# Attention and two feed-forward layers on one core: keys rotated by a block, half-empty blocks transposed in pairs, narrower value products

## The chip, the cores and the metric

The kernel runs on one core of a Trainium2 chip. The metric is device time in microseconds (us); the median of three timed runs is given, and the profile is of one further execution with its own time. Engines are named as the profile names them: PE (matrix products and transposes), PEld (its weight loads), DVE, ACT, POOL, and SP, which issues most DMA.

## The reference

```python
# q, k, v: (4, 8, 576, 64)  -> 32 heads of 576 positions, 9 blocks of 64
scores = (1.0 / np.sqrt(64)) * np.matmul(q, k.transpose(0, 1, 3, 2))
scores = np.where(pos[:, None] // 64 >= pos[None, :] // 64, scores, -1000000000.0)
attn = softmax(scores)                       # over the last axis
x = heads_side_by_side(np.matmul(attn, v))   # (2304, 512)
h = np.maximum(x @ w_in, 0.0);  x = h * h @ w_out            # d_ff 2048
h = x @ w_in2                                                # second layer
g = (a0 + a1 * h + a2 * h**2 + a3 * h**3) / (1 + abs(b0 * h) + abs(b1) * h**2 + 1e-6)
out = g @ w_out2
```

A query sees the keys of its own block of 64 and of all blocks before it.

## The kernel before, in words

**Queries.** Each head's 576 queries are padded in front with 64, which makes five tiles of 128 (t = 0 to 4). Tile t holds the query blocks 2t-1 and 2t. Its upper 64 rows see key blocks 0 to 2t, its lower 64 rows all of these but the last. So tile t has 128t + 64 columns of scores, and the last 64 of them are of use to the upper rows alone; for the others the score is masked.

**Slots.** A head is four slots (the table `GROUPS`): tiles 0 and 1 together, then tile 2, tile 3, tile 4. A slot passes through scores (`emit_s`, PE), row maxima (`emit_max`, DVE), exponentials with row sums (`emit_exp`, ACT, into tiles called p), scaling by the reciprocal of the sum (`emit_norm`, POOL), transposes of p in blocks of 128 by 128 through a PSUM tile tp (`emit_t`, PE), and copies into one tile pt that holds p with keys on the partitions. `emit_pv` then multiplies values by pt: half 0 covers the queries of tiles 0 to 2, half 1 those of tiles 3 and 4.

**Three rounds.** Heads 0 to 7 run in round one with slots 0 and 1 only and in round two with slots 2 and 3. Heads 8 to 31 run in round three with all four. Heads 0 to 9 are "plain": products in fp32, pt is `pt_plain`, one ACT copy per piece, and two heads share a value product's array side by side. The 22 others are "split": every number is a high and a low fp32r part, ACT copies the high part into pt and DVE writes the rest as the low part, and each value product is run for both (z = 0, 1).

**Buffers.** There are two sets of p tiles. The second lies in a pool `early` that is given up at the start of round three for `q_two` and `k_two`, so round three has one p tile for each t, whatever the head (`psets[un.hd % 2 if un.hd < H else 0]`; in the trace all are called p). pt exists once.

**Order.** `tc` schedules by a model of its own, so the order on every engine is the scheduler's; each engine then runs its list in order. Between the attention products PE runs the first half of the first feed-forward layer for the batch before (`moe_a`: tiles ha and ya, lines L482 and L495), a given number of steps for each slot. After attention come the rest of `moe_a` for the last batch, the second half of the layer (hb, yb) and the second layer (hc, yc). While attention runs, ACT, DVE and POOL also convert the layer's weights (tiles raw, cv, w).

Of the kernel before, what the change touches and what calls it, by code (L numbers as in the profile page):

```python
# [49 lines left out]
def attention_moe_moe(ctx: ExitStack, tc: tile.TileContext, q, k, v, wi1, wo1, wi2, wo2, a, b, out):  # L50
# [89 lines left out]
    early = tc.alloc_tile_pool(name="early", bufs=1)  # L140
    psets = []
    for pool in (attn, early):
        psets.append([])
        for t in range(5):
            w_ = P * (t + 1)
            pt_ = pool.tile([P, w_], F32, name=f"p{t}_{len(psets)}")
            nc.gpsimd.memset(pt_[:, w_ - D:w_], 0.0)
            if t == 0:
                nc.gpsimd.memset(pt_[0:D, 0:D], 0.0)
            psets[-1].append(pt_)  # L150


        nc.gpsimd.memset(psets[-1][3][:, D:P], 0.0)
        nc.gpsimd.memset(psets[-1][3][0:D, 0:D], 0.0)
        for n in (3, 4):
            nc.gpsimd.memset(psets[-1][n][:, SUB:SUB + D], 0.0)

    def ptile(un, t):
        own = psets[un.hd % 2 if un.hd < H else 0]
        if un.gis == (0, 1) and un.hd % 4 > 1:  # L160
            return own[4][:, 0:3 * P] if t == 2 else own[3][:, P * t:P * (2 * t + 1)]
        return own[t]

    pt = attn.tile([P, 2, 3, SP], F32, tag="pt", name="pt_plain", bufs=1)

# [6 lines left out]
    class Visit:  # L172
        def __init__(self, n, hd, at, gis):
            self.n, self.hd, self.plain, self.at, self.gis = n, hd, hd < PLAIN, at, gis

            self.scale = SCALE if n == 0 else 1.0

            self.q0, self.q1 = (0, 3 * P) if gis == (0, 1) else (3 * P, SP) if gis == (2, 3) else (0, SP)
            self.k1 = SUB if gis == (0, 1) else S

    def load_qk(un, eng=nc.sync):
# [8 lines left out]
        cuts = ((0, 256, 0, 192), (256, un.q1, 192, un.k1)) if un.n == 0 else ((un.q0, un.q1, 0, un.k1),)  # L190
# [9 lines left out]
    def make_two(un):  # L200
        early.release()
        late = tc.alloc_tile_pool(name="late", bufs=1, reuse_waits="tile")
        for n in range(2):
            q_two.append(late.tile([P, SP], F32R, name=f"q_two{n}"))
            k_two.append(late.tile([P, S], F32R, name=f"k_two{n}"))
            nc.scalar.activation(q_two[n][D:P], un.qr[D:P], AF.Copy)
            nc.scalar.activation(k_two[n][D:P], un.kr[D:P], AF.Copy)
        return late
# [57 lines left out]
    def emit_s(i):  # L266
# [12 lines left out]
        for t in g:  # L279
# [9 lines left out]
            else:  # L289
                o = D if t == 1 else 0  # L290
                parts = [(ps[:, o:o + w_], 0, w_)]
# [13 lines left out]
    def p_view(i, t):  # L305
        pv = ptile(slots[i][0], t)[D if t == 0 else 0:P, 0:P * t + D]
# [26 lines left out]
    def emit_norm(i):  # L333
# [19 lines left out]
        for n, t in enumerate(g):  # L353
            r = D if t == 0 else 0
            pv = ptile(slots[i][0], t)[r:P, 0:P * t + D]
            nc.gpsimd.tensor_scalar(pv, pv, st[r:P, 6 + n:7 + n], 0.0, op0=ALU.mult, op1=ALU.add)  # L356

    def emit_t(i):
# [3 lines left out]
        if un.hd == PLAIN and gi == 0:  # L362
            pt = attn.tile([P, 2, 3, SP], F32R, tag="pt", name="pt", bufs=1)
        un.pt = pt
        blocks = [(t, c) for t in g for c in range(t + 1)]
        for lo in range(0, len(blocks), 4):
            part = blocks[lo:lo + 4]
            ps = ps1.tile([P, 512], F32, tag="tp", name=f"tp{i}_{lo}", bufs=3)
            for n, (t, c) in enumerate(part):
                nc.tensor.transpose(ps[:, P * n:P * (n + 1)], ptile(slots[i][0], t)[:, P * c:P * (c + 1)], ident)  # L370
            t = g[-1]
            here, late = slice(P * t, P * (t + 1)), slice(P * (t - 3), P * (t - 2))

            if gi == 0:
                moves = [(slice(D, 2 * P), 0, slice(D, 2 * P)), (slice(2 * P, 3 * P), 1, slice(P, 2 * P))]
            elif lo:
                moves = [(slice(0, P), 1, slice(0, P))]
            else:
                moves = [(slice(0, 3 * P), None, here)]
                if gi > 1:  # L380
                    moves.append((slice(3 * P, 4 * P), 2, late))
            if un.plain:
                for src, c, cols in moves:
                    piece, dst = ps[:, src], un.pt[:, un.hd % 2, slice(0, 3) if c is None else c, cols]
                    if c is None:
                        piece = piece.rearrange("p (c j) -> p c j", j=P)
# [5 lines left out]
            ends = []  # L392
# [492 lines left out]
```

## Time and profile before

| | us |
|---|---|
| median of three runs | 1023.35 (1022.27 to 1026.43) |
| profiled execution, its own time | 1018.61 |
| its span, first to last instruction | 1016.8 |

A row of groups gives line, engine, operation, output<-inputs, shape and count, then busy us and mean ns of one, then idle us of the engine before them and what ended it. In a timeline each row begins with its start and its length in us. On PE, products follow each other while the earlier ones are still under way, so that the time one takes from its engine is the distance between starts, not its length. A fp32 product stands as two records in the trace, a transpose and a fp32r product as one.

### The profile page before, as it was taken

What the parts mean: (1) busy time and instruction counts of PE and PEld (TensorE: products, weight loads), DVE (VectorE), ACT (ScalarE), POOL (GpSimd) and SP (SyncE); (2) the same over time, 40 slices, a digit from 0 to 9 for tenths busy, and PEclk for the clock granted to TensorE, in tenths of its full rate; (3) what the DMA queues carried; (4) which work ended last, traced back from release to release, by engine and by line L of the source; (5) the groups of instructions that cost most, each with busy time, mean ns of one, the idle gap of its engine ahead of it and who ended that gap; (6) DMA issues with size and microseconds to landing.
All of it is one profiled execution on the core that took longest, in us unless ns stands there. A gap on an engine that the chain in (4) does not pass through costs nothing. (4 is left out here: it accounts for less than half of the span.)

```text
span 1016.8 us, 17069 instructions
## 1 busy us (share of the span) xinstructions
PE 995.1 (98%) x5721; PEld 882.6 (87%) x5721; DVE 741.8 (73%) x1412; ACT 728.5 (72%) x1620; POOL 591.1 (58%) x632
## 2 busy tenths in 40 slices
PE   7999999999999999999999999999999999999997
PEld 5678998999999999999888888887888888899996
DVE  6799688768787756676676756887766766777766
ACT  6789697768787746664555557887787776787775
POOL 4767686868786845630232448767556554655552
PEclk9999999999999999999999999999999999999999
DMA  8866435243332204567656572001101100100000
GB/s 268 253 195 216 128 97 154 88 114 116 119 93 81 67 24 141 191 193 256 231 166 200 172 242 88 1 1 42 41 1 32 42 1 1 57 17 1 32 1 31
DMA packets 63894, 106.58 MB, mean 105 GB/s; under 512 B 16064, under 2 KB 34496, under 8 KB 63808
## 3 DMA queue, kind: packets, MB, share of 16 engines
q1 hardware_dynamic: 63520, 105.34, 32.7%
q8 instruction: 45, 0.74, 0.3%
q14 instruction: 41, 0.34, 0.1%
q10 hardware_dynamic: 288, 0.16, 0.1%
HBM read 79.17 MB, written 23.07 MB: 101 GB/s over the span
## 5 line engine op out<-in xcount | busy, mean ns | idle before, releaser
L816 PE MATMUL yc<-w_co,gc 128*128 128x512 f32 x864 | 211.6, 391 | 2.9 <-ACT gc L776 2.9
L707 PE MATMUL hc<-xc,w_ci 128*128 128x512 f32 (+1 forms) x960 | 211.2, 368 | 0.0
L707 PEld LDWEIGHTS hc<-xc,w_ci 128*128 128x128 f32 x960 | 176.1, 188 | 26.3
L816 PEld LDWEIGHTS yc<-w_co,gc 128*128 128x128 f32 x864 | 161.2, 188 | 35.5 <-ACT gc L776 4.4
L777 POOL TENSOR_TENSOR gc<-t,gc 128x512 fp32r<-128x512 f32 (+1 forms) x78 | 105.1, 1353 | 126.1 <-issue 103.2
L482 PE MATMUL ha<-xt,w_ai 128*128 128x320 f32 (+1 forms) x768 | 122.5, 305 | 0.5 <-POOL xt L451 0.5
L495 PE MATMUL ya<-ga,w_ao 128*128 128x320 f32 (+1 forms) x768 | 116.8, 299 | 1.6 <-ACT r L508 0.9
L802 POOL TENSOR_TENSOR wq<-wq,ab 128x512 f32<-128x512 f32 (+1 forms) x78 | 96.3, 1235 | 28.6 <-ACT wq L800 28.6
L482 PEld LDWEIGHTS ha<-xt,w_ai 128*128 128x128 f32 x768 | 107.6, 189 | 5.1 <-issue 3.0
L495 PEld LDWEIGHTS ya<-ga,w_ao 128*128 128x128 f32 x768 | 106.5, 189 | 3.5 <-ACT r L508 1.1
L747 PE MATMUL yb<-gb,w_bo 128*128 128x512 f32 (+1 forms) x480 | 106.0, 368 | 0.0
L707 PE MATMUL hb<-xb,w_bi 128*128 128x512 f32 (+1 forms) x480 | 105.7, 368 | 0.0
L776 ACT ACTIVATE gc<-t 128x512 fp32r<-128x512 f32 (+1 forms) x80 | 47.1, 589 | 73.0 <-DVE t L785 72.9
L803 DVE TENSOR_TENSOR t<-hc,t 128x512 f32<-128x512 f32 (+1 forms) x80 | 50.9, 637 | 66.1 <-ACT t L801 66.1
L747 PEld LDWEIGHTS yb<-gb,w_bo 128*128 128x128 f32 x480 | 87.6, 188 | 12.0 <-DVE yp L752 0.3
L707 PEld LDWEIGHTS hb<-xb,w_bi 128*128 128x128 f32 x480 | 87.4, 188 | 11.3 <-ACT yo L500 0.2
L356 POOL TENSOR_SCALAR p<-p,stat 64x64 f32<-64x64 f32 (+4 forms) x110 | 64.4, 586 | 44.2 <-DVE stat L352 11.1
L402 DVE TENSOR_TENSOR pt<-tp,pt 128x128 fp32r<-128x128 f32 (+2 forms) x176 | 63.2, 391 | 27.0 <-ACT pt L400 16.6
L783 DVE SCALAR_TENSOR_TENSOR wq<-wq,ab 128x512 f32<-128x512 f32 (+1 forms) x80 | 54.9, 687 | 33.5 <-ACT ab L782 22.2
L370 PE MATMUL tp<-ident,p 128*128 128x128 f32 x480 | 77.8, 278 | 0.5 <-ACT xp L437 0.3
L400 ACT ACTIVATE pt<-tp 128x128 fp32r<-128x128 f32 (+2 forms) x176 | 57.1, 362 | 26.6 <-PE tp L370 25.0
L785 DVE SCALAR_TENSOR_TENSOR t<-t,coef,ab 128x512 f32<-128x512 f32 (+1 forms) x80 | 66.8, 835 | 1.7
(137 smaller groups left out, 2004.8 us busy)
## 6 DMA issues: line engine op xcount, KB each, us to landing
kr<-in_k_dram SPq DMA_DIRECT2D x32, 288.0 KB, 3.6
raw_ci<-in_wi_dram SPq DMA_DIRECT2D x16, 512.0 KB, 4.1
raw_co<-in_wo_dram SPq DMA_DIRECT2D x16, 512.0 KB, 3.9
qr<-in_q_dram SPq DMA_DIRECT2D x24, 320.0 KB, 3.3
raw_ai<-in_wi_dram SPq DMA_DIRECT2D x8, 512.0 KB, 5.1
raw_ao<-in_wo_dram SPq DMA_DIRECT2D x8, 512.0 KB, 4.0
raw_bi<-in_wi_dram SPq DMA_DIRECT2D x8, 512.0 KB, 3.4
raw_bo<-in_wo_dram SPq DMA_DIRECT2D x8, 512.0 KB, 3.5
```

What stands on the lines that cost most here:

```text
L356: nc.gpsimd.tensor_scalar(pv, pv, st[r:P, 6 + n:7 + n], 0.0, op0=ALU.mult, op1=ALU.add)
L370: nc.tensor.transpose(ps[:, P * n:P * (n + 1)], ptile(slots[i][0], t)[:, P * c:P * (c + 1)], ident)
L400: nc.scalar.activation(high, src, AF.Copy)
L402: nc.vector.tensor_tensor(low, src, f(high), op=ALU.subtract)
L482: nc.tensor.matmul(ps[:, 0:n], w[:, zw, P * kk:P * (kk + 1)], xt[:, zx, kk, first:end], start=i == 0, stop=i == 3 * KK - 1)
L495: nc.tensor.matmul(ps[:, 0:n], wA["o", m][:, zw, P * c:P * (c + 1)], gs[m][:, zg, 0:n], start=i == 0, stop=i == 3 * HALF - 1)
L707: nc.tensor.matmul(ps[:, 0:n], w[:, zw, P * kk:P * (kk + 1)], xt[:, zx, kk, 0:n], start=i == 0, stop=i == 3 * KK - 1)
L747: nc.tensor.matmul(acc[j, c][:, 0:n], wB["o", m][:, zw, P * c:P * (c + 1)], g[:, zg, 0:n], start=m == 0 and i == 0, stop=last and i == 2)
L777: (nc.vector if u - 2 >= len(units) - END else nc.gpsimd).tensor_tensor(g[:, 1, 0:n], t, f(g[:, 0, 0:n]), op=ALU.subtract)
L785: nc.vector.scalar_tensor_tensor(t, t, a0, r, op0=ALU.add, op1=ALU.mult)
L802: (nc.vector if u >= len(units) - END else nc.gpsimd).tensor_tensor(w, w, ab, op=ALU.mult)
L816: last = nc.tensor.matmul(acc[j, c], g[:, zg, P * c:P * (c + 1)], w3["o", m][:, zw, :], start=m == 0 and i == 0, stop=m == NM - 1 and i == 2)
```

## The change

1. The keys in memory are rolled by one block: column 0 holds block 8, then blocks 0 to 7. Tiles 0 to 3 read them from column 64 on. Tile 4 then has its half-used block first and not last.
2. p tiles lie side by side so that two half-used blocks of 64 columns share one 128 by 128 transpose: that of tile 0 with that of tile 1, that of tile 3 with that of tile 4. A head has 13 transposes instead of 15. A shared block is copied into pt in two pieces of 64 by 64, the second of them from partitions 64 to 127 to partitions 0 to 63; group (0, 1) has three copies instead of two, tile 3 one instead of two, tile 4 four instead of three.
3. The zeros that such copies no longer bring are written once into pt (`clear_pt`), and again when pt changes type at head 10.
4. Two sets of p tiles for tiles 0 to 2, three for tiles 3 and 4 in round two, two in round three. The pools `early` and `late` are gone.
5. Value products leave out columns whose p is zero: the two narrow ones of each half go from 256 and 128 columns to 192 and 64.

```diff
+    firsts = [attn.tile([P, 2 * P], F32, name=f"p01_{n}") for n in range(2)]
+    thirds = [attn.tile([P, 3 * P], F32, name=f"p2_{n}") for n in range(2)]
+    rests = [attn.tile([P, 8 * P], F32, name=f"p34_{n}") for n in range(3)]
...
+    def homes(un):
+        n = un.hd % 2
+        if un.gis == (0, 1):
+            if un.hd % 4 > 1:
+                return rests[n][:, 0:2 * P], rests[n][:, 2 * P:5 * P], None
+            return firsts[n], thirds[n], None
+        return firsts[n], thirds[n], rests[(un.hd + 2) % 3 if un.gis == (2, 3) else 1 - n]
...
+    def pblock(un, t, c):
+        first, third, rest = homes(un)
+        if t < 2:
+            return first[:, 0:P] if c < t else first[:, P:2 * P]
+        if t == 2:
+            return third[:, P * c:P * (c + 1)]
+        at = P * c if t == 3 else P * (c + 4)
+        return rest[:, at:at + P] if c < t else rest[:, 3 * P:4 * P]
...
-        blocks = [(t, c) for t in g for c in range(t + 1)]
+        t = g[-1]
+        blocks = [(t, c) for c in range(t + (t < 3))]
+        if t == 4:
+            blocks.append((4, 4))
+        up, low, mid = slice(0, D), slice(D, P), slice(P + D, 2 * P)
...
             if gi == 0:
-                moves = [(slice(D, 2 * P), 0, slice(D, 2 * P)), (slice(2 * P, 3 * P), 1, slice(P, 2 * P))]
+                moves = [(P, slice(0, P), 0, here), (up, mid, 1, mid), (low, mid, 0, low)]
             elif lo:
-                moves = [(slice(0, P), 1, slice(0, P))]
+                moves = [(up, low, 2, low), (low, low, 1, low)]
             else:
-                moves = [(slice(0, 3 * P), None, here)]
-                if gi > 1:
-                    moves.append((slice(3 * P, 4 * P), 2, late))
+                moves = [(P, slice(0, 3 * P), None, here)]
+                if t == 4:
+                    moves.append((P, slice(3 * P, 4 * P), 2, slice(P, 2 * P)))
...
     PV = (
-        ((0, D, 0, 320), (1, P, D, 256), (2, 2 * P, 192, P)),
-        ((0, 384, 0, 256), (1, 384, 0, 256), (2, 384, 0, 256), (3, 0, 0, 256), (4, 0, P, P)),
+        ((0, D, 0, 320), (1, P + D, P, 192), (2, 2 * P + D, 2 * P, D)),
+        ((0, 384, 0, 256), (1, 384, 0, 256), (2, 384, 0, 256), (3, D, D, 192), (4, D, P + D, D)),
     )
...
-        "k": stack(k, 0, MASKED),
+        "k": np.roll(stack(k, 0, MASKED), d_, axis=2),
```

The scheduler orders the instructions anew. Two places on PE show how.

PE in round three, from the last scores of slot 60 (head 15, tiles 0 and 1) on; tp is named by its slot. Before:

```order
L294 MATMUL sy60_2176<-k_two1_1140,q_two1_1139 128x192
L495 MATMUL ya0_1_0_2134<-ga0_1_4_1948,w_ao4_1100 128x256 x3
L495 MATMUL ya0_1_0_2134<-ga0_1_5_2013,w_ao5_1185 128x256 x3
L495 MATMUL ya0_1_0_2134<-ga0_1_6_2068,w_ao6_1264 128x256 x3
L370 MATMUL tp55_4_2106<-ident_70,p4_1_100 128x128
L442 MATMUL pv13_1_2142<-pt_1438,vs13_1931 128x256 x4
L442 MATMUL pv13_1_2142<-pt_1438,vs13_1931 128x128
L442 MATMUL pv13_1_2142<-pt_1438,vs13_1931 128x256 x4
L370 MATMUL tp56_0_2159<-ident_70,p0_1_91 128x128
L370 MATMUL tp56_0_2159<-ident_70,p1_1_94 128x128 x2
```

Of the change, the same place:

```order
L305 MATMUL sy60_2151<-k_two1_1113,q_two1_1112 128x192
L506 MATMUL ya0_1_0_2108<-ga0_1_4_1922,w_ao4_1077 128x256 x3
L506 MATMUL ya0_1_0_2108<-ga0_1_5_1988,w_ao5_1156 128x256 x3
L506 MATMUL ya0_1_0_2108<-ga0_1_6_2040,w_ao6_1236 128x256 x3
L387 MATMUL tp52_0_1945<-ident_70,p01_1_89 128x128 x2
L453 MATMUL pv12_1_1931<-pt_1409,vs12_1719 128x192
L453 MATMUL pv12_1_1931<-pt_1409,vs12_1719 128x64
L387 MATMUL tp53_0_1979<-ident_70,p2_1_91 128x128 x3
L305 MATMUL sx61_2182<-kk15_2000,qh15_1999 128x320
```

Before, the transposes of head 14 (slot 56, three of them) follow the scores of slot 60 and read the same p tiles that slot 60's exponentials write. Now those of head 13 stand there (slot 52, two of them), in a tile that slot 60 uses again after them; slot 56 comes later, from another tile.

PE at the end of attention, from the value product of head 31's first half on (ha3 is feed-forward work of the last batch). Before:

```order
L442 MATMUL pv31_0_5341<-pt_1438,vs31_5262 128x320
L442 MATMUL pv31_0_5341<-pt_1438,vs31_5262 128x256
L442 MATMUL pv31_0_5341<-pt_1438,vs31_5262 128x128
L370 MATMUL tp126_0_5354<-ident_70,p3_1_98 128x128
L370 MATMUL tp127_0_5379<-ident_70,p4_1_100 128x128 x4
L482 MATMUL ha3_0_1_5466<-xt3_4275,w_ai1_349 128x320
L482 MATMUL ha3_0_3_5506<-xt3_4275,w_ai3_512 128x320 x9
L370 MATMUL tp127_4_5388<-ident_70,p4_1_100 128x128
L482 MATMUL ha3_0_1_5466<-xt3_4275,w_ai1_349 128x320 x2
L482 MATMUL ha3_0_3_5506<-xt3_4275,w_ai3_512 128x320 x2
L442 MATMUL pv31_1_5404<-pt_1438,vs31_5262 128x256 x4
```

Of the change:

```order
L453 MATMUL pv31_0_5316<-pt_1409,vs31_5236 128x320
L453 MATMUL pv31_0_5316<-pt_1409,vs31_5236 128x192
L453 MATMUL pv31_0_5316<-pt_1409,vs31_5236 128x64
L387 MATMUL tp127_0_5351<-ident_70,p34_0_92 128x128 x4
L387 MATMUL tp127_4_5360<-ident_70,p34_0_92 128x128
L453 MATMUL pv31_1_5378<-pt_1409,vs31_5236 128x256 x3
L453 MATMUL pv31_1_5378<-pt_1409,vs31_5236 128x192
L453 MATMUL pv31_1_5378<-pt_1409,vs31_5236 128x64
L453 MATMUL pv31_1_5378<-pt_1409,vs31_5236 128x256 x3
L493 MATMUL ha3_0_1_5439<-xt3_4250,w_ai1_334 128x320 x2
```

The 14 feed-forward products that stood between head 31's last transposes and its last value product now stand elsewhere.

## Rows read from the trace of the kernel before

**Rows 1.** The page: span, and busy time by engine.
```profile
span 1016.8 us, 17069 instructions
PE 995.1 (98%) x5721; PEld 882.6 (87%) x5721; DVE 741.8 (73%) x1412; ACT 728.5 (72%) x1620; POOL 591.1 (58%) x632
```

**Rows 2.** Windows of 50 us: length, busy us (count) by engine, PE clock, DMA.
```profile
50.00:100.00 50.00, 49.41 (x319) 38.28 (x317) 47.52 (x80) 43.69 (x123) 35.64 (x39) 1.00 0.68 203
150.00:200.00 50.00, 46.42 (x358) 44.95 (x358) 40.11 (x116) 37.53 (x110) 35.78 (x49) 1.00 0.41 123
250.00:300.00 50.00, 50.00 (x394) 49.83 (x392) 40.30 (x115) 39.90 (x120) 39.32 (x55) 1.00 0.38 113
```

**Rows 3.** Windows of 10 us in round two, columns as in rows 2.
```profile
70.00:80.00 10.00, 10.00 (x65) 7.33 (x65) 9.78 (x19) 8.74 (x28) 6.37 (x8) 1.00 0.52 150
80.00:90.00 10.00, 9.41 (x67) 7.46 (x65) 9.49 (x16) 9.90 (x27) 5.48 (x6) 1.00 0.64 204
```

**Rows 4.** Timeline of PE: a run of five transposes.
```profile
44.56 0.71 PE L370 MATMUL tp<-ident,p 128*128 128x128 f32 x5
```

**Rows 5.** Timeline of PE in round three.
```profile
305.94 0.19 PE L294 MATMUL sy<-kk,qh 128*128 128x64 f32 x1
...
306.26 0.28 PE L294 MATMUL sy<-k_two,q_two 128*128 128x192 f32 x1
306.37 0.27 PE L370 MATMUL tp<-ident,p 128*128 128x128 f32 x1
...
307.07 0.64 PE L442 MATMUL pv<-pt,vs 128*128 128x256 f32 x4
307.54 1.04 PE L495 MATMUL ya<-ga,w_ao 128*128 128x320 f32 x6
308.42 0.49 PE L370 MATMUL tp<-ident,p 128*128 128x128 f32 x3
...
309.05 0.81 PE L442 MATMUL pv<-pt,vs 128*128 128x128 f32 x6
309.69 0.51 PE L370 MATMUL tp<-ident,p 128*128 128x128 f32 x3
```

**Rows 6.** Groups by line and shape, whole span.
```profile
L370 PE MATMUL tp<-ident,p 128*128 128x128 f32 x480 | 77.8, 278 | 0.5 <-ACT xp L437 0.3
L402 DVE TENSOR_TENSOR pt<-tp,pt 128x384 fp32r<-128x384 f32 x66 | 36.4, 552 | 16.7 <-PE tp L370 6.9 <-ACT pt L400 6.5 <-PE pv L442 2.3
L400 ACT ACTIVATE pt<-tp 128x384 fp32r<-128x384 f32 x66 | 32.3, 490 | 18.5 <-PE tp L370 17.6
L402 DVE TENSOR_TENSOR pt<-tp,pt 128x128 fp32r<-128x128 f32 x88 | 24.5, 280 | 2.8 <-ACT pt L400 2.7
L400 ACT ACTIVATE pt<-tp 128x128 fp32r<-128x128 f32 x88 | 24.1, 274 | 7.7 <-PE tp L370 7.4
L429 PE MATMUL pv<-pt_plain,vs 128*64 128x256 f32 x100 | 18.4, 390 | 0.0
L294 PE MATMUL sx<-kr,qr 128*128 128x288 f32 x40 | 11.6, 412 | 0.1
L294 PE MATMUL sy<-kr,qr 128*128 128x448 f32 x20 | 9.6, 564 | 0.5 <-ACT p L328 0.3
L445 ACT ACTIVATE tmp<-pv 64x320 f32<-64x320 f32 x22 | 9.5, 432 | 3.7 <-PE pv L442 3.2
```

**Rows 7.** What PE waited for from 150 to 200 us: us in total, times, longest.
```profile
PE sy L294 <- ACT p L328: 2.7, 2, 1.5
```

**Rows 8.** Timeline of all engines around the second of these waits.
```profile
180.88 0.49 PE L370 MATMUL tp<-ident,p 128*128 128x128 f32 x3
...
181.24 0.31 ACT L328 ACTIVATE p<-sy,stat 64x64 f32<-64x64 f32 x1 [3.47 <-issue]
...
183.29 0.47 PE L294 MATMUL sy<-kk,qh 128*128 128x448 f32 x1 [1.21 <-ACT p L328]
```

**Rows 9.** Timelines of POOL and PE at the start.
```profile
2.75 0.23 POOL L156 MEMSET p<- 128x64 f32 x2
...
3.58 2.48 PE L294 MATMUL sy<-kr,qr 128*128 128x64 f32 x6 [3.58 <-DMA kr<-in_k_dram]
```

More of the change, by code (lines that the diff above doesn't have):

```diff
@@ L158, in ptile @@
-    def ptile(un, t):
[L159 to L162, printed above, removed]
+    firsts = [attn.tile([P, 2 * P], F32, name=f"p01_{n}") for n in range(2)]
+    thirds = [attn.tile([P, 3 * P], F32, name=f"p2_{n}") for n in range(2)]
+    rests = [attn.tile([P, 8 * P], F32, name=f"p34_{n}") for n in range(3)]
+    for n in range(2):
+        for z, o in ((firsts[n], 0), (rests[n], 0)):
+            nc.gpsimd.memset(z[0:D, P + D:2 * P], 0.0)
+        for z, o in ((thirds[n], 0), (rests[n], 2 * P)):
+            nc.gpsimd.memset(z[:, o + SUB:o + 3 * P], 0.0)
@@ L164, in attention_moe_moe, with clear_pt @@
+    def ptile(un, t):
+        first, third, rest = homes(un)
+        if t < 2:
+            return first[:, 0:P + D] if t else first[:, P + D:2 * P]
+        return third[:, 0:SUB] if t == 2 else rest[:, 0:3 * P + D] if t == 3 else rest[:, 3 * P + D:8 * P]
+    def clear_pt(z):
+        nc.gpsimd.memset(z[D:P, :, 0, D:P], 0.0)
+        nc.gpsimd.memset(z[D:P, :, 1, D:2 * P], 0.0)
+        nc.gpsimd.memset(z[D:P, :, 2, D:P], 0.0)
     pt = attn.tile([P, 2, 3, SP], F32, tag="pt", name="pt_plain", bufs=1)
+    clear_pt(pt)
@@ L368, in emit_t @@
             ps = ps1.tile([P, 512], F32, tag="tp", name=f"tp{i}_{lo}", bufs=3)
[L369 to L372, printed above, removed]
+            for n, (_, c) in enumerate(part):
+                nc.tensor.transpose(ps[:, P * n:P * (n + 1)], pblock(un, t, c), ident)
             if gi == 0:
[L375 removed]
+                moves = [(P, slice(0, P), 0, here), (up, mid, 1, mid), (low, mid, 0, low)]
             elif lo:
[L377 removed]
+                moves = [(up, low, 2, low), (low, low, 1, low)]
             else:
[L379 to L381 removed]
+                moves = [(P, slice(0, 3 * P), None, here)]
+                if t == 4:
+                    moves.append((P, slice(3 * P, 4 * P), 2, slice(P, 2 * P)))
+            ends = []
+            for rows, src, c, cols in moves:
+                piece = ps[:, src] if rows is P else ps[rows, src]
+                dst = [(un.pt[:, z] if rows is P else un.pt[up, z])[:, slice(0, 3) if c is None else c, cols]
+                       for z in ((un.hd % 2,) if un.plain else range(2))]
+                ends.append((piece.rearrange("p (c j) -> p c j", j=P) if c is None else piece, dst))
             if un.plain:
[L383 to L386, printed above, removed]
+                for piece, (dst,) in ends:
                     if gi != 0 or un.hd < H:
@@ L601, in attention_moe_moe @@
         if i == 4 * PLAIN - 4:
-            late = make_two(slots[i][0])
+            make_two(slots[i][0])
         for back in range(4):
```

48 lines of the change are left out of this document (12 added, 36 removed).

## The prediction

> **What bounds the kernel now.** I read the page first: PE is busy for 98% of the span, and no other engine for more than 73% [rows 1]. A busy PE need not be a full one, so I read the windows next. From 250 to 300 us, with split heads in round three, PE has 394 products and transposes in 50 us and never pauses, while DVE, ACT and POOL have 10 us to spare each [rows 2]. There a product that goes away is time gained, and the feed-forward stages behind wait for PE alone. Two stretches of attention are different. From 50 to 100 us DVE is busy for 47.5 of 50 us, and PE gets only 319 products done [rows 2]; in round two DVE has 9.78 and 9.49, and ACT up to 9.90, of every 10 us [rows 3]. PE counts as busy there but is not the limit. And from 150 to 200 us PE stands idle for 3.6 us [rows 2], of which 2.7 are two waits of scores for an exponential [rows 7].
>
> **Transposes.** Two fewer for each of 32 heads: 64 of 480 [rows 6]. Their mean length of 278 ns is not what one costs, since they overlap. A run of three lasts 0.49 us and a run of five 0.71 [rows 4, 5], so one more makes the run (0.71 - 0.49) / 2 = 0.11 us longer. The 22 split heads all lie where PE is the limit: 44 x 0.11 = **4.8 us** gained. The 10 plain heads have 20 x 0.11 = 2.2, which I take up below.
>
> **Narrower products, split heads.** Each half has, for z = 0 and z = 1, a product of 256 columns that becomes 192 and one of 128 that becomes 64: 88 such pairs. Before: four products of 256 columns take 307.54 - 307.07 = 0.47, 0.117 each. A group of six, four of them of 256 columns and two of 128, takes 309.69 - 309.05 = 0.64, which leaves 0.085 for each of 128. A pair is 0.20. After: the scores of tiles 0 and 1 are products of just the new widths, two of 64 and two of 192 columns, and take 306.37 - 305.94 = 0.43, so 0.215 for a pair [rows 5]. The narrow pair is not cheaper. By these readings the edit is worth -0.015 x 88 = -1.3 us at worst. I take **0** and keep the other end, a gain in proportion to columns, for a rival: a pair loses 128 columns, and 128 columns are worth 0.117 - 0.085 = 0.032 between the old widths, so 0.032 x 88 = 2.8 us.
>
> The Trainium skill (TensorE: Matmul & The Clock Gate, section LDWEIGHTS (loading the stationary operand)) says that a weight load takes as many ns as it has columns divided by 1.2, whatever the contraction. Each of these products has its own 128 columns of weights, so by that rule of the Trainium skill each needs 107 ns however narrow it is, and the four products of the scores agree with it (0.43 / 4 = 0.107 us). The isolated gap of N / 2.4 + 2.5 ns on the same page of the Trainium skill (section Back-to-back issue gap) would make the edit worth 53 ns a pair, an estimate of 4.7 us; the four products speak against it.
>
> **Plain heads.** fp32 products are paid by columns: 448 against 288 columns is 564 against 412 ns a record, 0.95 ns a column, and each product has two records (100 records of 256 columns for 50 products) [rows 6]. 64 columns less in two products are 64 x 0.95 x 4 = 0.24 us for one half of one head. The two heads of a pair run side by side in the array; if they overlap wholly this counts once a pair, 5 pairs x 2 halves x 0.24 = 2.4 us, if not at all 4.9. I take 2.4. With the transposes that is 4.6. But the part in round two, one transpose in each of 8 heads and the second half of four pairs, 0.9 + 1.0 = 1.9, lies where DVE is the limit, and nothing in the change takes work from DVE there. So **2.7 us** counts (bounds 0, if the rest of round one waits for DVE and ACT as well, and 7.1).
>
> **Buffers.** At 181.24 the exponential of slot 60 starts after ACT has stood idle for 3.47 us; it follows at once on the three transposes at 180.88, those of the head before, which read the p tile that it writes; and the next scores, at 183.29, have waited 1.21 us for it [rows 8]. With two sets in round three the transposes that it must wait for are those of two heads earlier, which stand before. I count the two waits of this kind as gone: **2.7 us** (bounds 0, if PE then waits elsewhere, and the 3.6 us idle in that window).
>
> **The end of attention.** With the second set scores run further ahead, and the feed-forward work that is bound to slots goes with them. So the last heads' transposes and value products come when that filler is used up: 14 products that stood between head 31's transposes and its last product are gone from there. What is late next is the chain through the copies. From tile 2's transposes: high copy 0.49, low part 0.55, three products of 0.11, the copy tmp 0.43, two copies 0.49 and 0.27 [rows 6], together 2.6 us, in which PE has 14 products of its own, 1.5 us. That leaves 1.1 us of waiting, and about as much again for the low parts behind it (0.55, 0.28) and for the small copies. I count **-2 us** (bounds 0 and -4, if head 30 pays the same).
>
> **What I cost at nothing.** Copies: a split head has on ACT and on DVE nine instead of eight, but 1664 columns instead of 1856. A copy costs 274 ns for 128 and 490 for 384 columns on ACT, 280 and 552 on DVE [rows 6], so 0.84 and 1.06 ns a column with 0.17 and 0.14 fixed: +0.17 - 0.16 on ACT, +0.14 - 0.20 on DVE. Both engines have 10 us of 50 to spare there. The trace has no 64 by 64 copy with a shift of partitions; the copy of 128 by 128 bounds it from above and the fixed part from below. The rolled keys move the same bytes. The start-up zeros of POOL end before 3.0 us, hidden behind the key load that PE waits for until 3.58 [rows 9]; the new ones are fewer. The second set of zeros at head 10 is three POOL instructions ahead of copies that wait for the same value product anyway.
>
> **Sum.** 4.8 + 0 + 2.7 + 2.7 - 2.0 = 8.2 us off the span of 1016.8, so 1008.6, and 1010.4 with the 1.8 us that lie around it. The profiled execution, 1018.6, is 4.7 below the median of the timed runs; against 1023.35 the forecast is **1015.2 us**, faster by 0.8%. A difference under 0.5%, about 5 us, is what a measurement of this kernel can't tell from none.
>
> **Rivals.** (A) *Given back.* The round one part doesn't count (0), the waits move instead of going (0), and the tail costs 4: 4.8 - 4 leaves 1 us, 1022; with half of it, 4 us, 1019. For it: in round one PE is not full either. Against: rows 8 show a cause that is removed, not moved. (B) *Columns pay.* If the narrow products are priced by columns, 2.8 us more, and if the plain heads' saving counts in full, 1.9 more: 1010.5, with more waits gone 1009. The four products of the scores speak against it [rows 5]. (C) *Slower.* The last transpose of a head now feeds two copies on ACT and two on DVE, and the second half's value product stands right behind. If nothing lies between, every split head pays a further copy on each, at most 0.27 + 0.28 = 0.55: 12.1 us over 22 heads, the tail and no waits gained: 4.8 + 2.7 - 12.1 - 2 = -6.6, 1030. It decides from 8.2 / 22 = 0.37 us a head, where the gains of the sum are used up. Against: PE's list has feed-forward products there in all but the last heads, and PE never paused from 250 to 300 us with the same chain one copy shorter.
>
> **Chances.** Forecast 0.62, with a range of its own of 1012 to 1018; A 0.20; B 0.10; C 0.08. The forecast's cases and B are faster by more than 0.5% (below 1018.2), 0.72; A is no difference, 0.20; C is slower, 0.08. The range reaches up into A and down to B's end: 1009 to 1021.
>
> **What would show it.** 416 tp records, and three in a row still 0.49 us. The value products of 64 and 192 columns about 0.215 us a pair between starts; a pair at 0.17 or less would speak for B. In the window from 150 to 200 us, no wait of scores for an exponential. Round two as long as before, with DVE still over 9 of 10. Waits of value products for the copies of pt around the last two heads, some 2 us; such waits in every head would be C. Wrong I would be most likely in round one and two, where I share out the gain by which engine is full, and in the tail.

## The result, and the profile after

The change made the kernel slower: 1028.67 us median (12 runs, 1026.02 to 1031.04) against 1021.19 (12 runs) of before, a ratio of 1.0071 [1.0053, 1.0089]. The forecast was 1015.2 us, a ratio of 0.992. The profiled execution took 1030.96 us, and its span is 12.3 us longer than before; that is more than the 7.5 us between the medians, since the profiled execution of before lies 2.6 us below its median and that of the change 2.3 us above.

The page of the change; it answers to [rows 1].

```profile
span 1029.1 us, 16981 instructions
PE 993.8 (97%) x5657; PEld 880.1 (86%) x5657; DVE 754.5 (73%) x1436; ACT 732.1 (71%) x1650; POOL 594.3 (58%) x626
```

The same windows as [rows 2].

```profile
50.00:100.00 50.00, 47.26 (x300) 37.61 (x301) 47.15 (x83) 43.44 (x123) 34.88 (x39) 1.00 0.66 205
150.00:200.00 50.00, 45.40 (x320) 43.37 (x321) 41.29 (x119) 35.79 (x111) 33.74 (x45) 0.93 0.40 119
250.00:300.00 50.00, 48.79 (x376) 47.75 (x375) 41.03 (x123) 40.46 (x125) 38.23 (x53) 1.00 0.39 114
```

In each of them PE does fewer products than before (300 for 319, 320 for 358, 376 for 394) and is idle more. There is less work, and it is done at a lower pace. The view of waits gives part of the reason (us in total, times, longest; whole span):

```profile
PE tp L387 <- DVE pt L413: 4.1, 5, 2.7
PE sy L305 <- DMA kr<-in_k_dram: 3.7, 1, 3.7
PE yc L826 <- ACT gc L786: 2.9, 3, 1.6
PE sx L305 <- ACT p L339: 2.5, 3, 1.4
PE ya L506 <- ACT r L519: 2.2, 1, 2.2
PE yb L757 <- DVE yp L762: 2.0, 1, 2.0
PE pv L453 <- ACT pt L411: 1.6, 4, 0.8
PE pv L440 <- ACT pt_plain L406: 1.6, 3, 1.1
PE sx L305 <- DMA kr<-in_k_dram: 1.5, 1, 1.5
PE ya L506 <- POOL ga L523: 1.3, 3, 0.7
```

All rows of this view together are 29.7 us, and 16.4 before. Waits of split heads' transposes for copies of pt are new (4.1 us). Their value products (L453, before L442) wait 1.6 us for ACT's copies and another 1.0 for DVE's; before, it was 0.7 and 0.2:

```profile
PE pv L442 <- ACT pt L400: 0.7, 2, 0.4
...
PE pv L442 <- DVE pt L402: 0.2, 1, 0.2
```

The longest wait of the change for a copy of pt, in the timeline of PE and DVE (start, length):

```profile
169.87 1.60 PE L506 MATMUL ya<-ga,w_ao 128*128 128x256 f32 x12
...
171.30 0.49 PE L387 MATMUL tp<-ident,p 128*128 128x128 f32 x3
...
171.55 0.53 PE L453 MATMUL pv<-pt,vs 128*128 128x320 f32 x3
171.55 1.15 DVE L122 SCALAR_TENSOR_TENSOR cv_bo<-cv_bo,raw_bo 128x512 uint32<-128x512 uint32 x1
171.91 0.66 PE L387 MATMUL tp<-ident,p 128*128 128x128 f32 x4
172.62 0.74 DVE L326 TENSOR_REDUCE stat<-sx 128x1 f32<-128x576 f32 x1
173.29 1.35 DVE L249 SCALAR_TENSOR_TENSOR q_two<-qr,qh 64x640 fp32r<-64x640 f32 x1
...
174.64 0.53 DVE L413 TENSOR_TENSOR pt<-tp,pt 128x384 fp32r<-128x384 f32 x1
...
175.22 0.47 PE L387 MATMUL tp<-ident,p 128*128 128x128 f32 x1 [2.65 <-DVE pt L413]
...
175.71 2.05 PE L453 MATMUL pv<-pt,vs 128*128 128x256 f32 x8
```

From 171.30 until the next scores at 177.84 PE has transposes and value products alone, and no feed-forward product to fill the time. One wait stands among them, of 2.65 us. The copy at 174.64, which frees the PSUM tile tp for the transpose at 175.22 (there are three such tiles, shared with the value products), stands on DVE's list behind a conversion, a maximum and a q_two.

The first transposes, scores and products of three places, found in PE's timeline by counting off the slots (us from the start of the span). "Lead" is how many slots the scores are ahead of the last transposes that stand before them on PE's list, in most of round three.

| | lead | transposes of slot 31 | scores of 71 | of 126 | first hb | span |
|---|---|---|---|---|---|---|
| before | 4 to 5 | 79.6 | 184.5 | 346.0 | 415.7 | 1016.8 |
| change | 7 to 9 | 84.5 | 185.2 | 350.0 | 425.5 | 1029.1 |

In the change the scores of slot 71 come nearly as early as before (0.7 us later), but its transposes 9.5 us later (208.3, before 198.8). So at the end of attention more is left to do.

### The profile page after: what moved, and what is told of

Its sections match the earlier page's. It is cut to its first block, busy times and chain, and to the rows that moved or that the text cites. A ratio compares the mean times of both kernels' runs of the same rounds, so it can differ in the third digit from the quotient of the medians.

```text
span 1029.1 us, 16981 instructions
## 1 busy us (share of the span) xinstructions
PE 993.8 (97%) x5657; PEld 880.1 (86%) x5657; DVE 754.5 (73%) x1436; ACT 732.1 (71%) x1650; POOL 594.3 (58%) x626
## 5 line engine op out<-in xcount | busy, mean ns | idle before, releaser
L826 PEld LDWEIGHTS yc<-w_co,gc 128*128 128x128 f32 x864 | 161.3, 188 | 35.5 <-ACT gc L786 4.4
L367 POOL TENSOR_SCALAR p<-p,stat 64x64 f32<-64x64 f32 (+4 forms) x110 | 61.9, 567 | 37.5 <-DVE stat L363 11.7
L387 PE MATMUL tp<-ident,p 128*128 128x128 f32 x416 | 74.4, 286 | 7.0 <-DVE pt L413 4.1
L413 DVE TENSOR_TENSOR pt<-tp,pt 64x64 fp32r<-64x64 f32 (+2 forms) x198 | 64.1, 343 | 19.5 <-ACT pt L411 16.5
L411 ACT ACTIVATE pt<-tp 64x64 fp32r<-64x64 f32 (+2 forms) x198 | 58.2, 320 | 21.6 <-PE tp L387 18.7
```

The lines of the kernel that those rows point to most:

```text
L387: nc.tensor.transpose(ps[:, P * n:P * (n + 1)], pblock(un, t, c), ident)
L411: nc.scalar.activation(high, src, AF.Copy)
L413: nc.vector.tensor_tensor(low_, src, f(high), op=ALU.subtract)
L826: last = nc.tensor.matmul(acc[j, c], g[:, zg, P * c:P * (c + 1)], w3["o", m][:, zw, :], start=m == 0 and i == 0, stop=m == NM - 1 and i == 2)
```

## The experiments

All ratios are to the kernel before, on the same chip in the same comparison, with the 95% interval in brackets; the chip is not the same in every comparison. In every diff `turned[i]` is the last transpose of slot i, `copied[i]` its last ACT copy, and `tc.issue_after(x)` puts the block's instructions behind x on x's engine. Theory 1 was the lead: with a second set of p tiles the scheduler runs scores, and the feed-forward work bound to slots, ahead, and transposes and value products are left without filler (feed-forward products that keep PE busy meanwhile). Its rivals were the narrow products, and the changed copies.

**1. pairs_oldbuffers**: one set of p tiles in round three, two in round two.

```diff
-        return firsts[n], thirds[n], rests[(un.hd + 2) % 3 if un.gis == (2, 3) else 1 - n]
+        if un.gis == (2, 3):
+            return firsts[n], thirds[n], rests[n]
+        return firsts[0], thirds[0], rests[0]
```

With one set the next head's tile 3 is written over this head's last block of tile 3 before its transpose, since the shared transpose comes with tile 4; that block holds the next head's weights here. In this layout the pairing therefore needs the second set.

> The changed kernel with the buffers of before: two sets for tiles 3 and 4 in round two, one set of p tiles in round three; pairing, rolled keys and narrow products kept. In PE's list scores then stand again about 11 us of PE work ahead of the same slot's transposes, as before, and not 20. Theory 1 (the extra buffers let the scheduler run scores and feed-forward work ahead, so that transposes and value products come without filler and wait for copies): faster than before, ratio 0.985 to 0.995, waits of transposes and value products for copies of pt under 2 us in all, clock 1.00 in every window. Theory 2 (the paired blocks with their second small copy are what costs): as slow as the change, ratio about 1.007.

Measured: 1021.24, 1.0017 [1.0000, 1.0034], between what its two theories say. The loss is mostly gone, though the paired blocks and their small copies are all here; that speaks against theory 2. From slot 71's scores to slot 126's it takes 158.1 us (before 161.5), so the saving is there, but slot 71 starts 4.4 us later than before.

**2. old_twosets**: before, with a second set in round three and the pools `early` and `late` gone.

```diff
-        own = psets[un.hd % 2 if un.hd < H else 0]
+        own = psets[un.hd % 2]
-            q_two.append(late.tile([P, SP], F32R, name=f"q_two{n}"))
+            q_two.append(attn.tile([P, SP], F32R, name=f"q_two{n}"))
```

> The kernel before with a second set of p tiles in round three, and nothing else of the change: 15 transposes, wide products. Scores stand 16 to 26 us of PE work ahead of their transposes. Theory 1: slower than before, ratio 1.008 to 1.018, since nothing is saved and the waits of the change come; transposes wait for DVE copies of pt, and the clock falls somewhere. Theory 2: ratio 0.995 to 1.000, since the two waits of scores for an exponential (2.7 us) go and nothing comes.

Measured: 1042.57, 1.0214 [1.0163, 1.0265]. The buffers alone, with no pairing and no narrow product, cost more than the whole change, and more than theory 1 had said. From slot 71 to 126 it takes 176.3 us. The waits are not the ones expected: value products wait for DVE's xp, the sum that reads the value product before, and transposes wait for DVE's copies of pt for 0.8 us only. Some of its waits (view as above):

```profile
PE pv L438 <- DVE xp L442: 6.6, 4, 3.1
...
PE sy L290 <- ACT p L324: 3.8, 5, 1.5
...
PE yb L742 <- DVE yp L747: 2.3, 1, 2.3
PE ya L491 <- POOL ga L508: 2.3, 4, 1.2
```

**3. old_narrow**: before, with the narrow products alone (the second `PV` table of the diff on before's layout).

> The kernel before with the narrow value products alone (192 and 64 columns), transposes and buffers as before. By the prediction's reading a pair of narrow products in a split head takes what a wide pair takes, and the plain heads save some 2 us partly hidden: ratio 0.997 to 1.000. If columns are what is paid: 0.994 to 0.996.

Measured: 1023.12, 1.0027 [1.0003, 1.0050]. No gain, and the steady part from slot 71's scores to slot 126's takes 161.3 us (before 161.5). In the steady part the narrow products neither gain nor lose; where the 0.27% comes from is not shown.

**4. change_held**: the change, scores of round three put behind the transposes five slots back.

```diff
+            if i - 5 in turned and slots[i][0].hd >= H:
+                with tc.issue_after(turned[i - 5].ins):
                     emit_s(i)
```

> The changed kernel with all its buffers, but the scores of a slot in round three are put behind the transposes of five slots before, so that PE's list has before's distance (about 11 us of PE work) in spite of the buffers. Theory 1: faster than before, ratio 0.985 to 0.995, like the run with the old buffers. Theory 2: about 1.007. If the memory layout or the number of buffers itself cost something, this run is slower than the one with the old buffers.

Measured: 1019.78, 1.0001 [0.9980, 1.0023], not the 0.985 to 0.995 of theory 1. The loss is gone without touching a buffer or a copy. From slot 71 to 126 it takes 157.7 us, 3.8 less than before: there the saving is. PE is as full there as in [rows 2]:

```profile
250.00:300.00 50.00, 50.00 (x394) 49.86 (x393) 42.82 (x121) 40.79 (x128) 40.06 (x53) 1.00 0.40 113
```

But slot 71 starts at 188.0, 3.5 later than before. One window in the passage from round two to three shows a part of that; DVE is busy for 5.26 us, half of what it was there, and the granted clock is 0.83:

```profile
70.00:80.00 10.00, 8.40 (x48) 6.47 (x48) 5.26 (x13) 6.55 (x22) 4.40 (x6) 0.83 0.40 126
```

**5 to 7.** I took the hold's start for the cause, and tried it from slot 40 on (`i >= 40`), with seven slots instead of five, and slot by slot from 20 on by the distances that PE's list of before has (`turned[i - int(BACK[i - 20])]`, 3 to 6).

> The change, with the scores of slots 40 and later (split heads) put behind the transposes five slots back; slots before 40 as the scheduler of the change has them. Theory 1 (scores that run 8 to 10 slots ahead leave transposes and value products without filler; and the hold of the run change_held began too early, at the passage from round two to three, where DVE stood idle for 3.5 us and the clock was 0.83 from 70 to 80 us): 3 to 4 us less than change_held's 1.0001, 0.996 to 0.998. Theory 2 (the lead has no part in it beyond what change_held took back; what is left is lost in rounds one and two): 1.000.

> The same with seven slots in place of five. Theory 1, if the loss grows with the lead: between held_from_forty and the change (1.007), about 1.000 to 1.003. If only the lead of one head's length (four slots) more matters, as a threshold: equal to one of the two, 0.997 or 1.007.

> The change, with the scores of every slot from 20 on (rounds two and three) put behind the same slot's transposes as in the kernel before (3 to 6 slots back). Theory 1 for round two as well (its third buffer has the same effect there): rounds two and three as before but with less PE work, 4 to 8 us less than before, 0.992 to 0.996, with the scores of slot 63 about where they start before (159 us). Theory 2 (round one, and the changed copies, lose the time): scores of slot 63 some 2 to 4 us later than before, 0.997 to 1.001.

Measured: held_from_forty 1.0040 [1.0026, 1.0054], held_at_seven 1.0122 [1.0105, 1.0140], held_slot_by_slot 1.0045 [1.0032, 1.0059]. All three miss. Seven slots are worse than the change's own 7 to 9, so the loss does not simply grow with the lead. The first has the steady 157.7 us, but slot 71 only at 193.4; the third has slot 71 at 185.1, but 163.4 us for the steady part, where many of the odd slots are held at four. Something before slot 71 costs time that neither theory names.

**8, 9. light_before, light_change**: DVE's four instructions of each weight conversion on 64 columns, not 512.

```diff
+                low, high, cc, cu = low[:, 0:64], high[:, 0:64], c[:, 0:64], cu[:, 0:64]
-                nc.vector.tensor_scalar(c, c, 2.0, 122880.0 * 65536.0, op0=ALU.max, op1=ALU.min)
+                nc.vector.tensor_scalar(cc, cc, 2.0, 122880.0 * 65536.0, op0=ALU.max, op1=ALU.min)
```

> The kernel before, with the four DVE instructions of every weight conversion cut from 512 columns to 64 (and a scale that keeps the numbers small; the weights are then not the reference's). The control for light_change. By the window rows DVE is the limit in rounds one and two, so less DVE work there should free some 2 to 6 us: 0.994 to 0.998. If DVE's load is not what holds rounds one and two, 1.000.

> The change with the same cut of DVE's conversion work; the scores still run 8 to 9 slots ahead, as in the change. What counts is its ratio to light_before. Theory 1a (the lead does harm because copies without filler stand behind long conversions on DVE): with these short, the loss is gone and the PE work saved comes out, light_change / light_before 0.990 to 0.997. Theory 1b (the lead itself costs, by the chain of copies, whatever DVE does beside): 1.004 to 1.008, as with the full conversions.

Measured: 0.9918 [0.9905, 0.9931] and 1.0002 [0.9986, 1.0018], so light_change / light_before is 1.0085. The long conversions are not the cause: with them short the loss is as large, and from slot 71 to 126 it is 167.3 us against 158.8. Theory 1a falls. That leaves the lead itself, as 1b says; that the chain of copies is its path is not shown by this. light_before gained more than expected, and elsewhere: its transposes of slot 31 come at 79.9, as in the kernel before (79.6), so less work on DVE freed nothing up to there.

**10. held_mixed**: the distances of before up to slot 71, five slots from 72 on.

> The change, scores put behind the same slot's transposes as before in slots 20 to 71 (as in held_slot_by_slot, where slot 71 started 0.6 us later than before), and five slots back from 72 on (as in change_held, where slots 71 to 126 took 157.7 us, before 161.5, slot by slot 163.4). If the stretches add up: hb starts 0.6 - 3.8 + 1.7 = 1.5 us earlier than before, ratio 0.997 to 1.000. If an order in one stretch changes the next, 1.001 or more.

Measured: 0.9995 [0.9980, 1.0009]; the steady part 158.4, slot 71 at 185.5. The stretches add up about as expected.

**11, 12. split_only, split_only_wide**: the change for the split heads alone; the plain heads keep before's tiles, transposes, copies and products, and PE's list up to slot 35 is that of before. In the second the split heads' products are wide again. (In all split versions the end of head 9's tile 4 is overwritten by head 10's tile 3; in these two the split heads' mask also stands one block off. Instructions and shapes are as described.)

```diff
     def ptile(un, t):
+        if un.plain:
+            return old_tile(un, t)[:, 0:P * t + D]
```

> The change for the 22 split heads alone: the 10 plain heads keep the p tiles, the 15 transposes, the copies, the wide products and the unrolled keys of before, so that PE's list in rounds one and two is that of before; scores from slot 40 on stand behind the transposes five slots back. Theory P (what was saved in the plain heads comes back there as waits, by the order and the copies of the change): transposes of slot 31 at 79.6 us and scores of slot 71 at about 184.5, as before, then 3.8 us less up to slot 126 and 1 to 2 us more at the end of attention: 0.996 to 0.998. Its rival (the loss of 1 to 4 us before slot 71 belongs to round three itself): 1.000 or more, with the scores of slot 71 late by 1 us or more.

> split_only with the 88 pairs of narrow products at 256 and 128 columns again (the columns left out by the change are zeros in pt; three more of its corners are zeroed once). If a narrow pair is worth nothing, as the prediction took it: the same as split_only within 0.1%. If it is worth what starts in the trace of the change say (0.20 against 0.164 us a pair, 88 x 0.035): 3.1 us, 0.3%, slower than split_only.

Measured: 1.0037 [1.0018, 1.0055] and 1.0074 [1.0061, 1.0086]. Theory P fell: the transposes of slot 31 come at 84.0. PE's list is that of before up to 82.1; there before has these transposes next (at 79.6), and this run puts the scores of slot 36 and nine feed-forward products ahead of them. So 2.5 us were lost with the same list and 1.9 by the new order. That sent me to the other engines' lists, and there a second cause stood. ACT's timeline of split_only in round two:

```profile
64.91 1.25 ACT L231 ACTIVATE k_two<-kr 64x576 fp32r<-64x576 f32 x2 [1.01 <-DMA kr<-in_k_dram]
...
67.89 1.36 ACT L230 ACTIVATE q_two<-qr 64x640 fp32r<-64x640 f32 x2
69.27 0.83 ACT L430 ACTIVATE pt_plain<-tp 128x384 f32<-128x384 f32 x3
70.12 0.74 ACT L351 ACTIVATE p<-sx,stat 128x576 f32<-128x576 f32 x1
```

ACT's timeline of before has these copies here:

```profile
83.74 0.73 ACT L206 ACTIVATE q_two<-qr 64x640 fp32r<-64x640 f32 x1
84.38 0.67 ACT L207 ACTIVATE k_two<-kr 64x576 fp32r<-64x576 f32 x1
84.95 0.72 ACT L206 ACTIVATE q_two<-qr 64x640 fp32r<-64x640 f32 x1
85.58 0.67 ACT L207 ACTIVATE k_two<-kr 64x576 fp32r<-64x576 f32 x1
```

Before, q_two and k_two lay where the second set had been, so the copies had to wait for the end of round two. In the change they have room of their own, and the scheduler puts them there, at 65 to 69 us (in the change's own trace at 66.1 to 68.6), ahead of ACT's copies and exponentials in the stretch where ACT and DVE are the limit [rows 3].

**13. old_early_two**: before, with q_two and k_two in `attn` and the pools `early` and `late` gone; nothing else.

> The kernel before, with q_two and k_two in room of their own, as in the change, so that the four ACT copies that fill them (0.73 and 0.67 us each, 2.8 us) no longer wait for the p tiles of round two to be given up: ACT's list then has them in the middle of round two, before slot 29's exponential, and not behind its last copies. PE's list stays as it is. Theory Q (ACT is full in round two, so everything behind these copies is late by their length, and the passage to round three with it): transposes of slot 31 start at 83 to 84 us, not 79.6, and the time is 3 to 4.5 us longer, 1.003 to 1.0045. Rival (ACT has room for them, or PE makes it up in round three): 1.000 to 1.001.

Measured: 1025.38, 1.0046 [1.0031, 1.0061], at the upper end of theory Q. From slot 15's transposes to slot 31's it takes 47.9 us, before 44.2; the steady part is 161.5 us in both. Its copies, and what PE waits for behind them:

```profile
65.40 1.36 ACT L203 ACTIVATE q_two<-qr 64x640 fp32r<-64x640 f32 x2
66.77 0.83 ACT L384 ACTIVATE pt_plain<-tp 128x384 f32<-128x384 f32 x3
...
67.48 0.76 PE L366 MATMUL tp<-ident,p 128*128 128x128 f32 x5 [0.45 <-ACT pt_plain L384]
68.51 1.24 PE L290 MATMUL sx<-kr,qr 128*128 128x288 f32 x4 [0.26 <-ACT p L324]
```

But slot 31's transposes come at 81.5, not at 83 to 84, and PE's list did not stay as it was. At 79.62 PE is where it was in the kernel before, and goes on with the scores of slot 36:

```profile
79.62 0.71 PE L290 MATMUL sy<-kr,qr 128*128 128x64 f32 x4
...
81.49 0.71 PE L366 MATMUL tp<-ident,p 128*128 128x128 f32 x5
```

Before:

```profile
79.63 0.71 PE L370 MATMUL tp<-ident,p 128*128 128x128 f32 x5
```

Slot 15's transposes had come 1.8 us earlier, so of the 3.7 us 1.8 are lost on the same list and 1.9 by this order. What the early copies cost is shown; that all of it passes through a full ACT is not.

**14, 15, 16. change_late_two, forty_late_two, split_late_two**: the change, held_from_forty and split_only with the copies put back.

```diff
-            make_two(slots[i][0])
+            with tc.issue_after(copied[31].ins):
+                make_two(slots[i][0])
```

> The change, with those four copies put behind ACT's last copy of slot 31, as before; scores run ahead as in the change. Theory Q: 3 to 4 us less than the change's 1.0071: 1.003 to 1.004. Rival: 1.006 to 1.008.

> held_from_forty (1.0040) with the four copies put there as well: both causes undone, nothing else of the change touched. If they add up: 1.000 to 1.001. If the lead takes all by itself: 1.003 to 1.005.

> split_only (1.0037) with the four copies behind slot 31's last copy, in the place on ACT's list where before has them (k_two in two pieces each, as the keys of the plain heads are not rolled; the split heads' mask is then the right one again). PE's and ACT's lists up to slot 36 are those of before, so the transposes of slot 31 come at 79.6 us and slot 71's scores near 185; then 3.8 us less to slot 126, 1 to 2 more at the end of attention: 0.996 to 0.998. If round three takes back more: 0.999 to 1.001.

Measured: 1.0090 [1.0073, 1.0108], 1.0013 [0.9998, 1.0027], 0.9984 [0.9971, 0.9998]. With the scores held, the copies are worth 0.27% and 0.53%. forty_late_two has held_from_forty's list on PE until past slot 31 and gains 0.5 us from slot 15 to 31, but 5.9 from there to slot 71's scores. Without the hold nothing is gained, and both expectations miss: slot 71's scores start at 184.5, but its transposes still at 207.5. The third, split_late_two, lies between its two expectations; slot 71 comes at 188.4, and a value product has waited 2.67 us for DVE before, at 180.13.

**17, 18. mixed_late_two, split_best**: held_mixed with the copies put back; split_late_two with the distances of before up to slot 71.

> held_mixed (the whole change, scores held as in the kernel before up to slot 71 and five slots back after it, 0.9995) with the four copies into q_two and k_two behind ACT's copies of slot 31. If the two causes add up here as in forty_late_two (1.0040 to 1.0013): 2 to 3 us less, 0.9965 to 0.998, and slot 71's scores at 182 to 184 us, before the 184.5 of the kernel before. If the order of round two as the change has it eats that: 0.999 to 1.001.

> split_late_two (the change for the split heads alone, copies late, 0.9984) with the scores of slots 40 to 71 held as in the kernel before, not five slots back; five from 72 on. (One corner of the p tiles, left uncleared in split_only and split_late_two, is cleared.) There a value product waited 2.7 us for DVE at 180 us, which held_slot_by_slot and held_mixed don't show (0.7 at most). If that wait goes: 2 to 3 us less, 0.995 to 0.996. If another takes its place, as two waits for an exponential stand there before: 0.998.

Measured: **mixed_late_two 1016.01 us, 0.9968 [0.9954, 0.9981]**, split_best 0.9992 [0.9973, 1.0011]. The whole change with both side effects undone is faster than either kernel, as expected; the plain heads' part of it is worth having. split_best misses its 0.995 to 0.996: slot 71 comes at 184.6, 3.9 us earlier than in split_late_two, and the time is no shorter. The page of mixed_late_two:

```profile
span 1013.7 us, 16956 instructions
PE 986.1 (97%) x5657; PEld 875.5 (86%) x5657; DVE 752.2 (74%) x1436; ACT 729.4 (72%) x1650; POOL 592.8 (58%) x626
```

| | slot 31 | 71 | 126 | 71 to 126 | 126 to hb | first hb | ratio |
|---|---|---|---|---|---|---|---|
| before | 79.6 | 184.5 | 346.0 | 161.5 | 69.6 | 415.7 | |
| change | 84.5 | 185.2 | 350.0 | 164.8 | 75.5 | 425.5 | 1.0071 |
| change_held | 82.6 | 188.0 | 345.7 | 157.7 | 71.4 | 417.1 | 1.0001 |
| old_early_two | 81.5 | 188.7 | 350.2 | 161.5 | 69.4 | 419.5 | 1.0046 |
| forty_late_two | 82.6 | 186.1 | 343.8 | 157.7 | 72.0 | 415.8 | 1.0013 |
| mixed_late_two | 78.0 | 181.9 | 340.5 | 158.7 | 71.8 | 412.4 | 0.9968 |

Columns as in the table above (transposes of slot 31, scores of 71 and 126). Each time is of one profiled execution, the ratio is of all runs; executions of one kernel differ by some us (forty_late_two's profiled one is 3.3 us below its median).

## Why the prediction was wrong, step by step

**Transposes of split heads (4.8 us): right.** The change has 416 records of tp, as forecast. The 55 slots from 71 to 126 are 13.75 heads, 3.0 us at 0.22 a head; split_only_wide, with paired transposes and wide products, shows 161.5 - 158.0 = 3.5, a little more than the term.

**Narrower products (0): right by the stretch, with a rest.** From 71 to 126 the edit is worth 0.2 us alone (161.5 to 161.3) and 0.3 on top of the pairs (158.0 to 157.7). The sign that I named for rival B misled: a narrow pair takes less between its own starts (0.14 us on average from slot 71 to 126 of change_held, a wide one 0.20 before), but the transposes behind it take the difference back. PE's timeline of before, then of change_held:

```profile
276.04 0.48 PE L442 MATMUL pv<-pt,vs 128*128 128x320 f32 x3
276.36 0.62 PE L370 MATMUL tp<-ident,p 128*128 128x128 f32 x4
276.73 0.57 PE L442 MATMUL pv<-pt,vs 128*128 128x320 f32 x3
```

```profile
291.34 0.45 PE L453 MATMUL pv<-pt,vs 128*128 128x320 f32 x3
291.63 0.55 PE L387 MATMUL tp<-ident,p 128*128 128x128 f32 x3
291.93 0.54 PE L453 MATMUL pv<-pt,vs 128*128 128x320 f32 x3
```

Before: 276.73 - 276.04 = 0.69 for three products and four transposes, 0.58 without one transpose of 0.11. After: 291.93 - 291.34 = 0.59 for three products and three transposes. The products alone went from 0.32 to 0.29. That is 0.099 us for each of seven, and 0.098 for each of six: here a narrow product costs a place as a wide one does. The Trainium skill (TensorE: Matmul & The Clock Gate, section LDWEIGHTS (loading the stationary operand)) gives a weight load its columns divided by 1.2 as ns, which makes an estimate of 107 ns for each product with its 128 columns of weights, however narrow it is. The traces agree that the width of these products does not count here, but their mean of 0.098 us, with a product of 320 columns among them, lies some 8% below that estimate. What stays open: split_only_wide is 0.37% slower than split_only in the timed runs, which speaks for rival B, while old_narrow is 0.27% slower than before, which speaks against it. Only some 0.3 us of the first lies in the steady stretch and 0.9 at the end of attention; the profiled run of split_only was its slowest, so the profiles don't say where the rest is.

**Plain heads (2.7 us): about right in size, in the wrong place.** In mixed_late_two slot 31's transposes come 1.6 us and slot 71's scores 2.6 us earlier than before, and split_best, without this part, has slot 71 at 184.6 and is 0.24% slower than mixed_late_two. But I had the gain in round one and none in round two, as DVE is the limit there. In these traces it is the other way round: slot 15's transposes come at 37.5 (before 35.4), and from there to slot 31's it takes 40.6 us (before 44.2; in the change, with the copies early, 47.0). That the sum fits is luck in part, and slot 15 alone lies between 33.3 and 36.1 in the traces of kernels that keep the plain heads as before.

**Buffers (2.7 us gained): the step that failed.** I counted two waits of scores for an exponential as gone. They did shrink: of that kind 0.7 us is left from 150 to 200 us. But I priced the lead that this gives only at the tail. I had written that "scores run further ahead, and the feed-forward work that is bound to slots goes with them"; that holds all through round three, not only for the last heads. From 71 to 126 the change takes 164.8 us, held 157.7: 7.1 us. old_twosets shows the lead without the pairing (2.1%, and old_early_two gives 0.5% for the copies, which come early there too), change_held the pairing without the lead. How the lead costs the 7.1 us is shown in part only. By the view of waits 1.5 us are waits of value products in this stretch, for copies and for xp. By the distances between starts, transposes and value products take 4.9 us more in the change than held, these waits among them, feed-forward products 3.3 more (there are seven more of them) and scores 1.1 less; most of the 7.1 us is thus no idle time, but nearly the same work further apart. The range went wrong with it: its lower bound for this term was 0 "if PE then waits elsewhere", and rival C, which has the right kind of wait, tied it to longer copies and not to missing filler.

**A moved step that I did not cost.** Item 4 of the change says that the pools `early` and `late` are gone. I asked what the buffers free for the scores, not what else had been waiting for them: four copies on ACT, 0.73 + 0.67 + 0.72 + 0.67 = 2.8 us, which went 18 us ahead into round two, which I had myself found to be full. Alone they cost 0.46%, partly by the new order on PE that came with them.

**The end of attention (-2 us): too small in the change, and in the held kernels the right size without the cause.** From slot 126's scores to the first hb it is 69.6 us before and 75.5 in the change: 5.9 more, as the work held back by the lead comes on top; my bound was 4. The waits that I named as a sign are there around the last head, 0.65, 0.39 and 0.29 us at 368.14, 370.22 and 370.83, 1.3 in all where I said some 2, and for the first the profile names no copy. In change_held and mixed_late_two it is 71.4 and 71.8 us, 1.7 and 2.2 more. But there the scores don't run ahead, which my term rested on, and the waits are others: in change_held the feed-forward products ya wait 2.6 us for ACT and POOL there (before 1.5), a value product 0.25 for a copy of pt. That these come out near 2 is luck.

**Copies (0): right.** The 88 copies of 64 by 64 take 216 ns on ACT and 217 on DVE; with the wider ones that they replace, the split heads' copies of pt come to 0.3 us less on ACT and 1.0 less on DVE.

**Sum.** With both failures mended, the kernel takes 1016.0 against 1020.0 of before on that chip, some 3 to 4 us faster (by the ratio and by the medians); the sum without its buffer term was 4.8 + 2.7 - 2.0 = 5.5. That the lead and the early copies cost the change 1.0071 - 0.9968 = 1.0%, some 10.5 us, follows from their two ratios; the copies alone, with the lead left in, gave nothing back. What stays open: why seven slots are worse than the scheduler's own order, so that the lead in slots does not say what is lost; and the wait of yb for yp, 2.0 us after attention, in the change, change_held (1.7) and old_twosets (2.3), but not in mixed_late_two.

## What to carry to other kernels

A buffer that two things share is also an order. Before one is added or a shared place is split up, list everything that waited for it to be free, and ask where each would go if it came as early as its inputs allow; a scheduler will put it there, even into a stretch where its engine is the limit. More room for the head of a chain (scores) did not help here, where the tail (transposes, copies, value products) shares one engine with it: the filler was used up early and the tail came late. Hold the head to a distance, and measure that distance: five slots took the loss away in change_held, seven made it larger in held_at_seven.

## What the hardware showed that I had not expected

Towards the end of the wait of 2.65 us that ends at 175.22, TensorE's granted clock fell to 0.50, the 1.2 GHz level; it stayed there from 175 to 180 us, and rose again in the 5 us behind. Windows of the change, columns as in [rows 2]:

```profile
170.00:175.00 5.00, 2.57 (x23) 2.33 (x21) 5.00 (x9) 3.11 (x7) 3.81 (x6) 0.95 0.54 150
175.00:180.00 5.00, 4.76 (x20) 4.50 (x21) 3.76 (x15) 2.75 (x11) 1.06 (x2) 0.50 0.78 270
180.00:185.00 5.00, 5.00 (x35) 4.97 (x34) 3.44 (x13) 2.36 (x9) 2.84 (x6) 0.86 0.04 4
```

From 170 to 175 us PE was busy for 2.57 us, then got 20 products done in 5 us, and 35 in the next 5. So this wait was paid twice, as idle time and as slow products behind it. In old_twosets the same is seen from 280 to 300 us, around a wait of 3.08 us that ends at 288.49 (PE busy 6.71 of the first 10 us, clock 0.86 and then 0.80), and in split_late_two behind the wait of 2.67 us that ends at 180.13 (clock 0.50 from 180 to 186 us).
